# Hashed attention and a feed-forward on one core: queries are turned ahead of additions on VectorE, and normalizing and converting move into the phase on columns

## The chip, the core and the metric

The kernel runs on one core of a Trainium2 chip. The metric is the device time of one execution in microseconds. The profile is one execution taken by the hardware profiler; its times run from the first instruction. PE is TensorE's matmul, PEld its weight load, DVE is VectorE, ACT ScalarE, POOL GpSimd, and SP the engine that issues most transfers.

## What is computed

First comes attention over 4 batches and 8 heads, 768 positions of 64 numbers each. A query sees only keys with the same 6-bit hash. The result is then the input of a feed-forward with a gated activation.

```python
q_bits = (np.einsum('bhsd,dk->bhsk', q, proj) > 0)     # k likewise; 6 bits make a bucket
mask = q_bucket[:, :, :, None] == k_bucket[:, :, None, :]
scores = scale * np.matmul(q, k.transpose(0, 1, 3, 2))
scores = np.where(mask, scores, -1000000000.0)
attn = np.exp(scores - np.max(scores, axis=-1, keepdims=True))
attn = attn / (np.sum(attn, axis=-1, keepdims=True) + 1e-09)
x = np.matmul(attn, v)                                 # then (B,H,S,D) -> (B*S, H*D)
h = x @ w_in                                           # 3072x512 by 512x2048
out = (h * (1.0 / (1.0 + np.exp(-1.702 * h)))) @ w_out
```

## The kernel before

The kernel has two stages. The attention takes two heads at a time: a pair, one on partitions 0 to 63 and the other on 64 to 127. There are 16 pairs. The feed-forward follows; it multiplies matrices by a scheme of seven products in place of eight, and the change doesn't touch it.

Within a pair `n` the attention goes through these steps. The order of the calls is the order of the instructions on TensorE, VectorE, ScalarE and GpSimd (`manual_schedule`); each engine works through its own list in order and waits for the others by semaphores.

```python
def turn(n, name):                     # k or q, positions by features -> features by positions
    xt = xts[n, name] = wk.tile([P, S], F32, tag=f"{name}T", name=f"{name}T")   # 2 buffers
    nc.vector.transpose(xt, x.rearrange("p s i -> p (s i)"))

def hashed(n):                         # L408: four matmuls, on four groups of 32 columns of the array
    h = dots[n] = mps.tile([P, HS], F32, tag="m", name="hash")
    for i, x in enumerate("kq"):
        for c in range(2):
            r0 = D * i + 32 * c
            nc.tensor.matmul(h[r0 : r0 + 32, :], pf[x], xts[n, x][:, c * HS : (c + 1) * HS], ...)

def featured(n):                       # L413: bits as large numbers; eight small DMAs put them in place
    nc.vector.tensor_scalar(f, dots.pop(n), above[:, 0:1], weight[:, 0:1], op0=Alu.is_gt, op1=Alu.mult)
    ...
            queue.dma_start(out=feats[n % 2][x][...], in_=f[r0 : r0 + 2 * NB, :])

def scores(n, c, kts):                 # L432, L433; the feature product makes hidden scores very low
    for kt in kts:
        ps = sps.tile([P, 2, 512], F32, tag="s", name="ps")                    # 3 buffers
        ...                            # features (bf16), then queries by keys (f32)
        nc.scalar.activation(es[c][:, kt, :, 0:HS], ps[:, :, 0:HS], Act.Exp, scale=1.0 / D**0.5)

def add_low(n, c):                     # L440, L441: GpSimd adds three of six blocks of exponentials
    acc = accs[n, c, 0] = st.tile([P, 2, HS], F32, tag="acc0", name="acc0", bufs=1)
    nc.gpsimd.tensor_tensor(acc, es[c][:, 0, :, 0:HS], es[c][:, 1, :, 0:HS], op=Alu.add)
    nc.gpsimd.tensor_tensor(acc, acc, es[c][:, 2, :, 0:HS], op=Alu.add)

def add_high(n, c):                    # L446, L448: VectorE adds the other three, and GpSimd's sum
    nc.vector.scalar_tensor_tensor(acc, e[0], T * TINY, e[1], op0=Alu.add, op1=Alu.add)
    for x in (e[2], accs.pop((n, c, 0))):
        nc.vector.tensor_tensor(acc, acc, x, op=Alu.add)

def values(n, c, kts): ...             # L458: values by exponentials, in two halves c of the columns
def unload(n, c): ...                  # L469, L470: ScalarE writes them to xT
def total(n): ...                      # L479: sums over the keys, dn, four matmuls on four column groups

def invert(n):                         # 1/sum, laid out along the positions
    nc.vector.transpose(rt..., accs.pop(n))            # L485, reads dn
    nc.vector.reciprocal(r, ...)                       # L487, and L491 four times
    nc.vector.transpose(rs..., r...)                   # L493

def norm(n):                           # L498
    nc.vector.tensor_tensor(x, x, rs.rearrange("p (t s) -> p t s", t=T), op=Alu.mult)
```

Beside this a generator `convert` turns one block of the float64 weight `w_in` into float32. Each `step` issues one VectorE instruction of it, six in all: L178, L182, L186 (ahead of which ScalarE squares the high word, L190, once L182 has read it), L193, L195, L198.

The loop over the pairs, from the second on:

```python
for n in range(1, last + 1):
    scores(n, 0, every)
    add_low(n, 0)
    if n == 1:
        add_high(0, 1); turn(2, "k"); total(0)
    invert(n - 1)
    norm(n - 1)
    if 1 < n < last:
        turn(n + 1, "k")
    scores(n, 1, every)
    add_low(n, 1)
    add_high(n, 0)
    if n < last:
        turn(n + 1, "q")
        hashed(n + 1)
        featured(n + 1)
        ...                            # ScalarE measures k and q, for a guard on large inputs
    else:
        guard(0); guard(1)
    step(n, 2)
    add_high(n, 1)
    values(n, 0, every); unload(n, 0)
    step(n, 4)
    values(n, 1, every); unload(n, 1)
    total(n)
    ...                                # transfers: k and q of n + 2, v and a weight block of n + 1
```

So TensorE's order in a pair is twelve score blocks (72 instructions), the hash of the next pair (8), the values (48), dn (8). The raw k and q have one buffer each; a transfer into it waits until the turn and the measurement of the pair before have read it.

Of the kernel before, what the change touches and what calls it, by code (L numbers as in the profile page):

```python
# [38 lines left out]
def kernel(  # L39
# [243 lines left out]
    def attention(ff):  # L283
# [4 lines left out]
        with actx:  # L288
# [99 lines left out]
            def turn(n, name):  # L388
                x = raws[n, name]
                xt = xts[n, name] = wk.tile([P, S], F32, tag=f"{name}T", name=f"{name}T")  # L390
                nc.vector.transpose(xt, x.rearrange("p s i -> p (s i)"))  # L391

            def measure(n, name):

                x = raws.pop((n, name))
                i = 2 * n + "kq".index(name)
                junk = st.tile([P, S], BF16, tag="junk", name="junk", bufs=1)
                nc.scalar.activation(junk, x.rearrange("p s i -> p (s i)"), Act.Square, accum_out=sizes[:, i : i + 1])
# [3 lines left out]
            def hashed(n):  # L402
# [5 lines that stand above are left out]
                        nc.tensor.matmul(h[r0 : r0 + 32, :], pf[x], xts[n, x][:, c * HS : (c + 1) * HS],  # L408
                                         start=True, stop=True)

            def featured(n):
                f = wk.tile([P, HS], BF16, tag="f", name="f", bufs=1)
# [4 lines that stand above are left out]
                        queue = nc.scalar if (n, x, c) == (1, "q", 0) else nc.sync  # L417
                        for j in range(2):
                            r0 = D * i + 32 * c + 2 * NB * j
                            queue.dma_start(out=feats[n % 2][x][D * j : D * j + 2 * NB, c * HS : (c + 1) * HS],  # L420
                                            in_=f[r0 : r0 + 2 * NB, :])

            def scores(n, c, kts):
                qT, kT, qf, kf = xts[n, "q"], xts[n, "k"], feats[n % 2]["q"], feats[n % 2]["k"]
                cols = slice(c * HS, (c + 1) * HS)
                for kt in kts:
                    ps = sps.tile([P, 2, 512], F32, tag="s", name="ps")
                    keys = slice(kt * P, (kt + 1) * P)
                    for a, m, last in ((kf, qf, False), (kT, qT, True)):
                        for j in range(2):  # L430
                            hs = slice(D * j, D * (j + 1))
                            nc.tensor.matmul(ps[:, j, 0:HS], a[hs, keys], m[hs, cols], start=not last, stop=last)  # L432
                    nc.scalar.activation(es[c][:, kt, :, 0:HS], ps[:, :, 0:HS], Act.Exp, scale=1.0 / D**0.5)  # L433
# [3 lines left out]
            def add_low(n, c):  # L437
# [5 lines that stand above are left out]
            def add_high(n, c):  # L443
                e = [es[c][:, GT + i, :, 0:HS] for i in range(GT)]
                acc = accs[n, c] = st.tile([P, 2, HS], F32, tag="acc", name="acc")
# [3 lines that stand above are left out]
# [12 lines left out]
            def x_of(n):  # L461
                b, hp = pairs[n]
                x = xT[:, hp, b * S : (b + 1) * S]
                return x.rearrange("d (t p) -> d t p", p=P) if n else x.rearrange("d (p t) -> d t p", p=P)

            def unload(n, c):
                av = avs.pop((n, c))
                vs = st.tile([P, 1], F32, tag="vs", name="vs")
                nc.scalar.copy(vs, av[:, HS : HS + 1])  # L469
                nc.scalar.activation(x_of(n)[:, c * GT : (c + 1) * GT, :], av[:, 0:HS].rearrange("p (t s) -> p t s", t=GT), Act.Identity, bias=vs[:, 0:1])  # L470

            def total(n):

                dn = accs[n] = aps.tile([P, HS], F32, tag="av", name="dn")
                for c in range(2):
                    acc = accs.pop((n, c))
                    for j in range(2):
                        r0 = D * j + 32 * c
                        nc.tensor.matmul(dn[r0 : r0 + 32, :], ones[:, 0:32], acc[:, j, :], start=True, stop=True)  # L479

            def invert(n):


                rt = st.tile([P, HS // 32, 32], F32, tag="rt", name="rt", bufs=1)
                nc.vector.transpose(rt.rearrange("p s i -> p (s i)"), accs.pop(n))  # L485
                r = st.tile([P, 2, HS // 32], F32, tag="r", name="r")
                nc.vector.reciprocal(r, rt[:, :, 0].unsqueeze(1).to_broadcast([P, 2, HS // 32]))  # L487
                for r0 in range(0, P, 32):
                    c = r0 // 32 % 2
                    r1 = r0 + 32 - 64 * c  # L490
                    nc.vector.reciprocal(r[r1 : r1 + 32, c], rt[r0 : r0 + 32, :, 0])  # L491
                rs = accs[n] = st.tile([P, S], F32, tag="rs", name="rs", bufs=1)
                nc.vector.transpose(rs.rearrange("p (s i) -> p s i", i=32),  # L493
                                    r.rearrange("p c s -> p (c s)").unsqueeze(2).to_broadcast([P, S // 32, 32]))

            def norm(n):
                x, rs = x_of(n), accs.pop(n)
                nc.vector.tensor_tensor(x, x, rs.rearrange("p (t s) -> p t s", t=T), op=Alu.mult)  # L498

            last = len(pairs) - 1  # L500
            conv = {}

            def step(n, count=1):
                for _ in range(count):
                    next(conv.get(n, iter(())), None)
# [9 lines left out]
            def guard(part):  # L515
                if part == 0:
                    nc.vector.tensor_reduce(largest, sizes, axis=AX.X, op=Alu.max)
                else:
                    row = mps.tile([1, P], F32, tag="m", name="row")
                    nc.tensor.transpose(row, largest, ident)  # L520
                    nc.vector.tensor_reduce(largest[0:1, 0:1], row, axis=AX.X, op=Alu.max)
# [30 lines left out]
# [4 lines that stand above are left out]
                    add_high(0, 1)  # L556
                    turn(2, "k")
                    total(0)
                invert(n - 1)
                norm(n - 1)  # L560
                if 1 < n < last:
                    turn(n + 1, "k")
                scores(n, 1, every)
                add_low(n, 1)
                add_high(n, 0)
                if n < last:
                    turn(n + 1, "q")
                    hashed(n + 1)
                    featured(n + 1)
                    for x in "kq":  # L570
                        measure(n + 1, x)
                else:
                    guard(0)
                    guard(1)
                step(n, 2)
                add_high(n, 1)
                values(n, 0, every)
                unload(n, 0)
                step(n, 4)
                values(n, 1, every)  # L580
                unload(n, 1)
                total(n)
                if n + 2 <= last:
                    for x in "kq":
                        fetch(n + 2, x)
                if n < last:
                    fetch_v(n + 1)
                    begin(n + 1)
                if n > last - len(x_sums):
                    x_sums[n - last - 1]()  # L590
            for f in in_sums(0):
                f()
            early.close()
            next(ff)
            invert(last)
            norm(last)


# [370 lines left out]
    def whole(steps):  # L969
        for _ in steps:  # L970
            pass
# [46 lines left out]
```

## Time and profile before

| what | us |
|---|---|
| time, median of three runs | 888.33 |
| the three runs | 886.65 to 888.75 |
| span of the profiled execution | 886.9 |
| attention, to the end of the last dn | 335.4 |
| first product of the feed-forward (L705) | 288.6 |
| second product and the output | 262.9 |

The granted TensorE clock averages 0.995 of full speed. In the attention TensorE is busy 330.6 us of 335.4, VectorE 280.7, ScalarE 214.5 and GpSimd 123.6. In the feed-forward's first product TensorE is busy all of the 288.6 us.

The views used are the page (busy times, shares, the costliest groups), the chain of work that ended last in order of time, the timeline (each row a start, a length, an engine, a line, and in brackets the idle time before it with what ended it) and busy times by stretch. A matmul's busy time runs up to the next matmul where the two follow closely, so a wait inside a group of matmuls can show only as a longer group.

### The profile page before, as it was taken

The page shows a single profiled execution, that of the slowest core. Times are in us where ns is not written, and L with a number is a line of the kernel's source. Part 1 is how long each engine was busy: PE and PEld are TensorE (multiplying, and loading weights), DVE is VectorE, ACT ScalarE, POOL GpSimd, SP SyncE. Part 2 cuts the span into 40 slices and gives each one's busy share as a digit, 9 for nine tenths or more (in the row PEclk, how much of TensorE's full clock was granted, in tenths as well). Part 3 has the DMA queues.
Part 4 walks back from the last instruction along what each step waited for, and adds up shares of the span by engine and source line. Part 5 has one row for each costly group of instructions (what it writes and reads, how often), then busy time and mean ns, then how long its engine had stood idle before and what let it go on. Part 6 is the DMA issues. An engine that isn't in the chain of part 4 may idle for free.

```text
span 886.9 us, 11860 instructions
## 1 busy us (share of the span) xinstructions
PE 873.2 (98%) x4077; PEld 502.7 (57%) x4077; DVE 722.4 (81%) x1020; ACT 313.9 (35%) x519; POOL 319.0 (36%) x275
## 2 busy tenths in 40 slices
PE   9999999999999999999999999999999999999996
PEld 4444444444444444444444444444888888888885
DVE  4568989999998997777787786898797977897786
ACT  5746566666666652332222323222100000000000
POOL 4234333334334346666444435559913100000000
PEclk9999999999999999999999999999999999999998
DMA  5334444555544402555555545565845585477524
GB/s 131 58 57 81 82 83 82 94 97 99 110 83 82 82 27 84 202 182 198 190 195 201 191 161 199 198 219 197 296 183 190 167 223 214 163 221 238 198 97 98
DMA packets 169157, 132.00 MB, mean 149 GB/s; under 512 B 123617, under 2 KB 138113, under 8 KB 163713
## 3 DMA queue, kind: packets, MB, share of 16 engines
q1 hardware_dynamic: 166528, 129.70, 50.7%
q10 hardware_dynamic: 2560, 1.46, 0.8%
q8 instruction: 34, 0.56, 0.3%
q14 instruction: 35, 0.28, 0.1%
HBM read 79.69 MB, written 50.33 MB: 147 GB/s over the span
## 4 chain that ended last, share of the span: by engine, by line
PE 94%; DVE 4%; issue 1%; DMA 0%; ACTq 0%; DVEq 0%; ACT 0%
PE product L705 33%; PE product L817 27%; PE ps L432 16%; PE av L458 14%; PE hash L408 2%; PE dn L479 1%; DVE xT L821 1%; PE tp L366 1%; DVE y L797 1%; DVE acc L448 0%; DVE acc L446 0%; DMA k<-in_k_dram 0%; PE hash L373 0%; DVE rs L493 0%; DVE qT L391 0%
## 5 line engine op out<-in xcount | busy, mean ns | idle before, releaser
L433 ACT ACTIVATE e<-ps 128x768 f32<-128x768 f32 x192 | 151.5, 812 | 24.3 <-PE ps L432 21.9
L432 PE MATMUL ps<-qT,kT 64*128 64x384 f32 x768 | 155.1, 482 | 0.0
L705 PE MATMUL product<-xT,w_in_sb 128*128 128x512 f32 x288 | 135.4, 592 | 0.0
L458 PE MATMUL av<-e,v 128*64 128x385 f32 x768 | 129.1, 491 | 0.0
L440 POOL TENSOR_TENSOR acc<-e 128x768 f32<-128x768 f32 x32 | 49.3, 1541 | 206.6 <-ACT e L433 155.5
L713 ACT ACTIVATE c<-c 128x512 f32<-128x512 f32 x72 | 45.4, 630 | 186.2 <-issue 71.8
L458 PEld LDWEIGHTS av<-e,v 128*64 128x64 f32 x768 | 54.0, 136 | 74.1 <-issue 70.7
L705 PEld LDWEIGHTS product<-xT,w_in_sb 128*128 128x128 f32 x288 | 54.6, 190 | 69.0 <-issue 64.5
L705 PE MATMUL product<-t_x,s_in 128*128 128x512 f32 x192 | 90.2, 592 | 0.0
L432 PEld LDWEIGHTS ps<-qT,kT 64*128 64x128 f32 x768 | 68.0, 187 | 38.7 <-issue 38.7
L219 POOL TENSOR_TENSOR v<-c,u 128x512 f32<-128x512 f32 x24 | 34.2, 1425 | 123.3 <-ACT c L713 123.3
L830 ACT COPY u<-product 128x256 f32<-128x256 f32 x21 | 7.8, 373 | 172.1 <-PE product L817 138.9
L441 POOL TENSOR_TENSOR acc<-acc,e 128x768 f32<-128x768 f32 x32 | 62.7, 1960 | 2.5
L432 PE MATMUL ps<-qf,kf 64*128 64x384 bf16 x384 | 62.8, 324 | 0.1
L705 PEld LDWEIGHTS product<-t_x,s_in 128*128 128x128 f32 x192 | 36.5, 190 | 45.9 <-issue 43.3
L705 PE MATMUL product<-xT,s_in 128*128 128x512 f32 x96 | 45.1, 592 | 0.0
L705 PE MATMUL product<-t_x,w_in_sb 128*128 128x512 f32 x96 | 45.1, 592 | 0.0
L446 DVE SCALAR_TENSOR_TENSOR acc<-e 128x768 f32<-128x768 f32 x32 | 40.3, 1261 | 5.1 <-ACT e L433 5.1
L432 PEld LDWEIGHTS <-kf 64*128 64x128 bf16 x384 | 18.8, 94 | 35.1 <-issue 11.1
L469 ACT COPY vs<-av 128x1 f32<-128x1 f32 x32 | 5.1, 159 | 89.2 <-PE av L458 89.2
L817 PE MATMUL product<-raw_g,xT 128*128 128x256 f32 x152 | 35.1, 379 | 0.0
L448 DVE TENSOR_TENSOR acc<-acc,acc 128x768 f32<-128x768 f32 x32 | 31.0, 969 | 3.7 <-DVE acc L448 0.5
(207 smaller groups left out, 1535.4 us busy)
## 6 DMA issues: line engine op xcount, KB each, us to landing
raw_g<-g_dram SPq DMA_DIRECT2D x22, 1024.0 KB
s_in<-g_dram SPq DMA_DIRECT2D x20, 1024.0 KB
g_dram<-c SPq DMA_DIRECT2D x72, 256.0 KB
g_dram<-t SPq DMA_DIRECT2D x48, 256.0 KB
raw<-in_moe_w_in_dram SPq DMA_DIRECT2D x16, 512.0 KB
raw<-in_moe_w_out_dram SPq DMA_DIRECT2D x16, 512.0 KB
v<-in_v_dram SPq DMA_DIRECT2D x32, 192.0 KB
g_dram<-u SPq DMA_DIRECT2D x24, 256.0 KB
```

What stands on the lines that cost most here:

```text
L219: return [lambda: eng.tensor_tensor(t1, b12, b11, op=Alu.subtract), lambda: eng.tensor_tensor(b12, b22, b12, op=Alu.subtract), lambda: eng ...
L408: nc.tensor.matmul(h[r0 : r0 + 32, :], pf[x], xts[n, x][:, c * HS : (c + 1) * HS], start=True, stop=True)
L432: nc.tensor.matmul(ps[:, j, 0:HS], a[hs, keys], m[hs, cols], start=not last, stop=last)
L433: nc.scalar.activation(es[c][:, kt, :, 0:HS], ps[:, :, 0:HS], Act.Exp, scale=1.0 / D**0.5)
L440: nc.gpsimd.tensor_tensor(acc, es[c][:, 0, :, 0:HS], es[c][:, 1, :, 0:HS], op=Alu.add)
L441: nc.gpsimd.tensor_tensor(acc, acc, es[c][:, 2, :, 0:HS], op=Alu.add)
L446: nc.vector.scalar_tensor_tensor(acc, e[0], T * TINY, e[1], op0=Alu.add, op1=Alu.add)
L448: nc.vector.tensor_tensor(acc, acc, x, op=Alu.add)
L458: nc.tensor.matmul(av[D * j : D * (j + 1), :], vt[:, t, j, :], es[c][:, t, j, :], start=(t == 0), stop=(t == T - 1))
L705: nc.tensor.matmul(ps, wq[LEFT[i]][:, kc, :], xq[RIGHT[i]][:, kc, :], start=(kc == 0), stop=(kc == K2 - 1))
L713: nc.scalar.activation(c, c, Act.Gelu_apprx_sigmoid)
L817: nc.tensor.matmul(ps, wq[LEFT[i]][:, c, :], gq[RIGHT[i]][:, c, :], start=(c == 0), stop=(c == F4 - 1))
```

## The change

VectorE's order within a pair is changed. The first transpose of `invert` stays at the front, so that dn's buffer comes free; then the keys are turned, then the rest of `invert` runs. The queries of the next pair are turned ahead of the first additions. `norm` moves behind the hash and its features, and all six steps of the conversion move behind the second additions, that is, into the time in which TensorE multiplies values. The aim is that the turned queries, which TensorE's hash needs, don't stand behind work that nobody waits for. No instruction is added or left out, and the order of the other engines stays. In the last pair, which has no next one, norm moves behind the guard.

```diff
@@ invert @@
                 nc.vector.transpose(rt.rearrange("p s i -> p (s i)"), accs.pop(n))
+                yield
                 r = st.tile([P, 2, HS // 32], F32, tag="r", name="r")
...
@@ the loop over the pairs @@
-                invert(n - 1)
-                norm(n - 1)
+                inverted = invert(n - 1)
+                next(inverted)
                 if 1 < n < last:
                     turn(n + 1, "k")
+                whole(inverted)
                 scores(n, 1, every)
                 add_low(n, 1)
+                if n < last:
+                    turn(n + 1, "q")
                 add_high(n, 0)
                 if n < last:
-                    turn(n + 1, "q")
                     hashed(n + 1)
                     featured(n + 1)
...
                 else:
                     guard(0)
                     guard(1)
-                step(n, 2)
+                norm(n - 1)
                 add_high(n, 1)
                 values(n, 0, every)
                 unload(n, 0)
-                step(n, 4)
+                step(n, 6)
                 values(n, 1, every)
                 unload(n, 1)
                 total(n)
...
-            invert(last)
+            whole(invert(last))
             norm(last)
```

`whole` runs a generator to its end. For n = 1 the keys of pair 2 are turned ahead of `total(0)` in both kernels.

## The prediction

> **What bounds the kernel now.** I read the page first: busy times, then the engines of the chain that ended last.
>
> ```profile
> PE 873.2 (98%) x4077; PEld 502.7 (57%) x4077; DVE 722.4 (81%) x1020; ACT 313.9 (35%) x519; POOL 319.0 (36%) x275
> ...
> PE 94%; DVE 4%; issue 1%; DMA 0%; ACTq 0%; DVEq 0%; ACT 0%
> ```
>
> TensorE is the bound, and a reordering on VectorE (DVE) can pay only where TensorE is held up or runs below its rate. "Busy 98%" hides such places, because a matmul's end is modelled and stretches up to the next one. So I read the chain in order of time (start, length, what) and compared the length of the same work in different places.
>
> ```profile
> 23.45 0.78 PE hash L408 x8
> ...
> 45.06 1.49 PE hash L408 x4
> 46.56 8.76 PE av L458 x48
> ...
> 196.36 9.80 PE ps L432 x72
> 206.15 1.49 PE hash L408 x8
> 207.64 7.92 PE av L458 x48
> 215.56 0.78 PE dn L479 x8
> ```
>
> The eight hash instructions took 0.78 us at 23.45, where keys and queries were both ready, but 1.49 at 206.15. The four sums into dn, with the same shapes and the same four column groups, always take 0.78. So 0.71 us is lost in the hash of a pair in the steady state. A pair there takes 9.80 + 1.49 + 7.92 + 0.78 = 19.99 us, and this repeats from n = 2 to 14. Only n = 4 to 5 is longer, with one period about 0.35 us over.
>
> The timeline of that stretch names the holder (start, length, then the idle time before and its releaser):
>
> ```profile
> 199.41 1.96 DVE L498 TENSOR_TENSOR xT<-xT,rs 128x768 f32<-128x768 f32 x1
> ...
> 205.78 0.97 DVE L391 STREAM_TRANSPOSE qT<-q 128x768 f32<-128x768 f32 x1
> 206.00 1.54 POOL L440 TENSOR_TENSOR acc<-e 128x768 f32<-128x768 f32 x1 [3.08 <-DVE acc L448]
> 206.08 0.14 PEld L408 LDWEIGHTS hash<-kT,pf_k 128*32 128x32 f32 x4 [0.55 <-DVE acc L448]
> ...
> 206.80 0.14 PEld L408 LDWEIGHTS hash<-qT,pf_q 128*32 128x32 f32 x4 [0.58 <-DVE qT L391]
> ...
> 207.69 0.68 DVE L413 TENSOR_SCALAR f<-hash,above,weight 128x384 bf16<-128x384 f32 x1 [0.94 <-PE hash L408]
> ```
>
> The turn of q ends at 206.75 and the q half of the hash starts at 206.80. The k half was through by then, so the halves run one after the other. The turn stands behind three additions, and those behind the normalization.
>
> The first pair of the loop, n = 1, is worse. I cut its 19.58 us by clock (us, busy, granted clock, DMA share, GB/s):
>
> ```profile
> 35.74:41.41 5.67, 5.67 (x46) 1.00 0.31 63
> 41.41:45.06 3.65, 0.84 (x6) 0.97 0.02 4
> 45.06:46.50 1.44, 1.44 (x6) 0.50 0.00 0
> 46.50:50.50 4.00, 4.00 (x22) 0.78 0.03 7
> 50.50:55.32 4.82, 4.82 (x34) 1.00 0.18 33
> ```
>
> TensorE stands for 2.8 us before the q half, and then it runs at half clock to about 48.
>
> **What the Trainium skill says.** "TensorEngine Tiling (Array Packing)", Key Properties: tiles work independently and in parallel. The 0.78 against 1.49 agrees: four column tiles together take about as long as two. "TensorE: Matmul & The Clock Gate", What's actually happening: the array falls to half clock after an idle window of some 3.4 us and needs a busy one to return. The 0.50 after 2.8 us of standing agrees in kind; the idle time here is shorter. "SBUF — State Buffer", Who interferes with whom: a VectorE instruction with two SBUF inputs contends with a GpSimd one that reads SBUF, one with a single input doesn't. The trace agrees: beside GpSimd's additions the normalization took 1.96 us and the first addition 1.54 (0.95 alone), while the turn of k at 201.29 kept its 0.96.
>
> **The change, part by part.** No instruction is added or removed; only VectorE's order differs (ScalarE, GpSimd and TensorE keep theirs).
>
> *Order within a pair.* Before: rt, r, rs, norm, kT, three additions, qT, f, two conversion steps, three additions, four conversion steps. After: rt, kT, r, rs, qT, three additions, f, norm, three additions, six conversion steps.
>
> *Steady state, TensorE.* Measured from the end of dn, qT is done after 0.1 + 0.58 + 0.96 + 0.30 + 0.92 + 0.98 + 0.97 = 4.8 us and gaps, say 5. TensorE asks for it 9.80 us after dn. Even 4 us of lag doesn't hold it, so the hash falls to 0.78 and the period to 9.80 + 0.78 + 7.92 + 0.78 = 19.28. Pairs n = 2 to 14 hash a next one: 13 x 0.71 = 9.2 us.
>
> *n = 1.* The inversion runs from 36.59 to 39.49. The turn of q(2) can follow at once and end at 40.5: its transfer was issued at 30.0 to 32.2, and the DMA share falls to 0.02 from 38 us. The hash, due at 41.41, then ends at 42.19, the values take 7.92 without the slow clock, and dn starts at 50.1 instead of 55.3: 5.2 us. (2.8 standing, 0.7 for the overlap, 0.75 slow hash, 0.9 slow values.) The second additions must be through for dn. On VectorE: first additions to 43.6, f to 44.3, norm (1.56) to 45.9, additions (1.2 + 0.96 + 0.96) to about 49.3, after GpSimd's sum at about 46.9. That is in time by 0.8.
>
> *n = 4 and 15.* The late period (0.35) and the last dn (1.07 instead of 0.78, waiting for an addition) go too: 0.6 us.
>
> *What I add back.* The period of 19.28 comes close to VectorE's own. Its busy time from 196.42 to 216.41 sums to 18.7, and 0.35 of gaps makes 19.05. The change moves L178 out of GpSimd's way (1.57 to about 0.69), so I estimate 18 to 19: it fits, with little room. The second loop is the transfer: from the end of f, 6.1 us to issue eight feature DMAs, then k with 2.2 us of issue. The 393 KB of k, counted at the rates 129, 172, 175 GB/s from 195.6, are across at 198.1: 9.7 after f's end at 188.39. Behind that kT 1.0, r and rs 2.3, qT 1.0, additions 3.6, f 0.7: 18.3, and up to 19.4 if completion takes a microsecond more. So f may slide by 0.1 to 0.3 us a pair. The first 1 to 1.5 us cost nothing: the additions for dn have 7.2 us after f and need 5.6. Estimate of the loss: 0.7 us.
>
> The sum: 9.2 + 5.2 + 0.6 - 0.7 = 14.3; 888.3 - 14.3 = 874.0 us, 1.6% less. From 335 us on the kernel is the same: 288.6 us of TensorE without a gap, then the second product.
>
> **The rivals.** *VectorE becomes the bound.* For it: the busy sum of 18.7 in 19.99, and normalization that may still meet GpSimd's addition, now right after f. If its period came to 19.7, only 0.28 x 13 = 3.7 of the 9.2 us would remain, and with n = 1 the time would be about 879. Against it: 0.94 us of idle ahead of f, and two long overlaps with GpSimd become one or one and a half.
>
> *The transfer of k takes the place of the wait.* kT now comes after 0.6 us of the pair instead of 5, and everything behind it waits too, since VectorE works in order. For it: k is across 1.8 us after dn's end at 196.3. Against it: the q turn has 4 us of room, f's features about 3. If completions lie well over a microsecond behind the last byte, the period is 19.5 to 19.8 and the time 876 to 880.
>
> *The exponentials are held up.* The square of the weights on ScalarE (L190) waits for L182, now about 1 us before dn rather than 5 after the hash; the last unload and the next pair's exponentials stand behind it. With six such 0.6 us slips the loss would be 4 us: 878. Against it: three score buffers allow TensorE 2.4 us, and the square should be done 0.3 us before dn ends.
>
> *No effect.* If the hash were long for another reason (the switch of tile shapes, say), only n = 1 would gain: 883. The 0.78 at 23.45 speaks against it.
>
> **Range and chances.** Low end: no loss, and the shortest of the three runs before was 1.7 under the median: 871.5. High end: one rival in half its strength, 878.5. Two per cent less is 870.6, which needs more than every loss I found. Faster by over 2%: 0.05. Within 2%: 0.93. Slower: 0.02, for a wait I didn't see.
>
> **What would show it.** Right: hash at 0.78 in the chain from n = 2 to 14, and periods of 19.3; no stretch near 45 us at clock 0.50, dn of n = 1 near 50; dn of the last pair near 320 instead of 334.3; idle time of VectorE ahead of f, released by the hash; kT with up to 2 us of idle before it. Wrong: periods of 19.6 or more with dn waiting for an addition (VectorE or the transfer), ps waiting for e (ScalarE), or a longer stretch after the attention.

## The result, and the profile after

| | median us | runs, from to |
|---|---|---|
| before | 888.54 | 886.65 to 888.82 |
| after | 877.48 | 876.77 to 877.59 |

The ratio is 0.9878, with a 95% interval of 0.9861 to 0.9895: 11 us less. The predicted 874.0 was 3.5 us too low; the range of 871.5 to 878.5 holds the result. The span of the profiled execution fell from 886.9 to 875.0.

The page of the changed kernel, the lines that answer to those shown of before: busy times, and the engines of the chain that ended last.

```profile
PE 861.9 (99%) x4077; PEld 502.7 (57%) x4077; DVE 719.6 (82%) x1020; ACT 310.2 (35%) x519; POOL 321.3 (37%) x275
...
PE 90%; DVE 6%; SPq 1%; DMA 1%; issue 1%; ACT 0%; ACTq 0%; DVEq 0%
```

TensorE's busy time fell by 11.3 us although it executes the same 4077 instructions: what went away is the time in which the two halves of the hash ran one after the other, each booked as work, and 1.6 us of work at half clock. VectorE has a larger part of the chain than before, a first sign that it now ends some waits. The chain in order of time (start, length, what) says where:

```profile
35.48 0.78 PE dn L479 x8
...
46.60 2.23 DVE acc L446
...
50.99 0.84 PE dn L479 x4
51.84 9.80 PE ps L432 x72
61.63 0.78 PE hash L408 x8
62.41 7.92 PE av L458 x48
70.33 0.78 PE dn L479 x8
...
313.67 0.11 DVE largest L518
313.81 0.27 PE row L521
314.09 7.92 PE av L458 x48
322.00 0.78 PE dn L479 x8
322.78 288.60 PE product L708 x672
```

(The dn at 35.48 is that of n = 0.) Three things are to be seen. The hash takes 0.78 us in place of 1.49, and a pair takes 9.80 + 0.78 + 7.92 + 0.78 = 19.28. The dn of the first pair of the loop comes at 50.99, in two halves: the line shown is the second one, and VectorE's additions (L446, L448) lead up to it. And near 313.7 the chain passes from VectorE's L518 to TensorE: a new wait. The feed-forward's first product takes 288.60 us as before.

Where the time came from, from one dn to another: from the first dn to the end of the last took 335.36 - 35.74 = 299.6 us before and 322.78 - 35.48 = 287.3 after. Of these 12.3 us, 9.2 come from thirteen hashes, 4.0 from the pair n = 1 (19.58 to 15.58), 0.6 from the late period and the last dn, and 1.5 were lost at L518.

The clock in the pair n = 1, to compare with the stretches shown of before (us, busy, granted clock, DMA share, GB/s):

```profile
41.20:45.00 3.80, 3.80 (x30) 1.00 0.01 4
45.00:46.50 1.50, 1.50 (x12) 1.00 0.05 12
46.50:50.50 4.00, 4.00 (x26) 1.00 0.05 12
```

TensorE no longer stands, and the clock stays at 1.00. But the timeline of the same pair shows what follows:

```profile
43.61 1.54 POOL L440 TENSOR_TENSOR acc<-e 128x768 f32<-128x768 f32 x1 [7.12 <-DVE acc L448]
...
43.98 2.62 DVE L499 TENSOR_TENSOR xT<-xT,rs 128x768 f32<-128x768 f32 x1
...
45.23 2.77 POOL L441 TENSOR_TENSOR acc<-acc,e 128x768 f32<-128x768 f32 x1
...
46.42 2.39 DVE L446 SCALAR_TENSOR_TENSOR acc<-e 128x768 f32<-128x768 f32 x1
...
50.99 0.84 PE L479 MATMUL dn<-acc,ones 128*32 128x384 f32 x4 [0.31 <-DVE acc L448]
```

VectorE and GpSimd take turns by whole instructions: the normalization waits for L440 to end, L441 then for the normalization, L446 for L441. So normalization and the first addition took 5.0 us together in place of my 2.8, the additions ended at 50.94 in place of 49.3, and the second half of dn waited 0.31 us after the first. It then ran by itself for 0.84 us, where both halves together take 0.78: 1.1 us lost in all.

The last pair, at the row of the guard:

```profile
307.83 0.57 DVE L485 STREAM_TRANSPOSE rt<-dn 128x384 f32<-128x384 f32 x1
...
313.58 0.18 DVE L518 TENSOR_REDUCE largest<-sizes 128x1 f32<-128x32 f32 x1
...
313.81 0.27 PE L521 MATMUL row<-ident,largest 128*1 128x128 f32 x1 [1.52 <-DVE largest L518]
```

VectorE begins this pair (rt) 5.4 us after the dn before it. In the middle pairs it begins 2 to 3 us after dn, because the conversion now all stands behind the additions; here L221, a sum for the feed-forward, comes on top, and takes 2.57 us beside GpSimd. L518 stands behind the three first additions, and TensorE waits 1.52 us for it.

### The profile page after: what moved, and what is told of

Read it like the earlier page. It is cut to its first block, busy times and chain, and to the rows that moved or that the text cites. A ratio compares the mean times of both kernels' runs of the same rounds, so it can differ in the third digit from the quotient of the medians.

```text
span 875.0 us, 11818 instructions
## 1 busy us (share of the span) xinstructions
PE 861.9 (99%) x4077; PEld 502.7 (57%) x4077; DVE 719.6 (82%) x1020; ACT 310.2 (35%) x519; POOL 321.3 (37%) x275
## 4 chain that ended last, share of the span: by engine, by line
PE 90%; DVE 6%; SPq 1%; DMA 1%; issue 1%; ACT 0%; ACTq 0%; DVEq 0%
PE product L708 33%; PE product L820 27%; PE ps L432 16%; PE av L458 12%; PE dn L479 1%; PE hash L408 1%; DVE acc L448 1%; DVE acc L446 1%; DVE xT L824 1%; SPq L420 1%; DVE y L800 1%; DVE xT L499 1%; DMA pj<-in_proj_dram 0%; DMA k<-in_k_dram 0%; DVE t_x L221 0%
## 5 line engine op out<-in xcount | busy, mean ns | idle before, releaser
L433 ACT ACTIVATE e<-ps 128x768 f32<-128x768 f32 x192 | 149.0, 813 | 15.7 <-PE ps L432 13.7
L440 POOL TENSOR_TENSOR acc<-e 128x768 f32<-128x768 f32 x32 | 50.4, 1575 | 192.2 <-ACT e L433 113.4
L441 POOL TENSOR_TENSOR acc<-acc,e 128x768 f32<-128x768 f32 x32 | 64.1, 2002 | 2.5
L446 DVE SCALAR_TENSOR_TENSOR acc<-e 128x768 f32<-128x768 f32 x32 | 52.1, 1628 | 5.1 <-ACT e L433 5.1
L448 DVE TENSOR_TENSOR acc<-acc,e 128x768 f32<-128x768 f32 x32 | 31.0, 969 | 3.8 <-ACT e L433 0.5
L448 DVE TENSOR_TENSOR acc<-acc,acc 128x768 f32<-128x768 f32 x32 | 31.0, 969 | 3.3
```

## The experiments

Times are medians; ratios, with their 95% intervals, are to the kernel before on the same chip, which took 888.1 to 888.9 us beside these runs. A period is the time from the end of one dn to the end of the next; steady pairs of the changed kernel have 19.28 us.

**e1: only the turn of q.** The kernel before, with

```diff
+                if n < last:
+                    turn(n + 1, "q")
                 add_high(n, 0)
                 if n < last:
-                    turn(n + 1, "q")
                     hashed(n + 1)
```

> The kernel before with one part of the change: the turn of the next queries moves ahead of the first additions; normalization and conversion stay where they were. Theory (the turn of q is all that TensorE waits for): from the end of dn the turn ends after some 7 us, still ahead of the 9.8 us at which the hash is due, so hash 0.78 us in nearly all pairs, 13 x 0.71 = 9.2 us; for n = 1 the turn ends near 42.1, TensorE stands under 1 us and keeps its clock, about 4.4 us; sum 13.6, some 875 us. Rival (VectorE becomes the bound unless normalization and conversion get out of GpSimd's way): the period goes to about 19.6 instead of 19.28, a third to a half of the gain is lost, 879 to 881 us, and dn waits for additions.

Measured: 882.01 us, ratio 0.9936 (0.9916 to 0.9957). The hash is at 0.78 from n = 2 on, so the theory holds for TensorE's wait; but only 6 of the 11 us come. Its timeline, VectorE in a steady pair and what dn waits for:

```profile
201.33 0.67 DVE L413 TENSOR_SCALAR f<-hash,above,weight 128x384 bf16<-128x384 f32 x1
201.92 1.73 DVE L178 SCALAR_TENSOR_TENSOR w_in_sb<-raw,mask_3fffffff 128x512 uint32<-128x512 uint32 x1
203.69 2.06 DVE L182 SCALAR_TENSOR_TENSOR bits<-raw,w_in_sb 128x512 uint32<-128x512 uint32 x1
205.67 0.95 DVE L446 SCALAR_TENSOR_TENSOR acc<-e 128x768 f32<-128x768 f32 x1
...
208.79 0.14 PEld L479 LDWEIGHTS dn<-acc,ones 128*32 128x32 f32 x4 [0.29 <-DVE acc L448]
```

The features no longer wait for the hash: VectorE works without a pause, period 19.70. The two conversion steps meet GpSimd (1.73 and 2.06 in place of 0.69 each) ahead of the additions, and the second half of dn waits in every pair. The rival is what happened, and a little more of it than it said: with the hash fast, VectorE's order behind it sets the period.

**e2: the turn of q undone.** The changed kernel with that same part back.

> The changed kernel with that one part undone: the queries are turned behind the first additions again; keys, normalization and conversion stay in their new places. Theory (the turn of q is what matters): VectorE begins a pair some 2 us after dn's end, the turn then ends about 9.9 us after dn or later, so the hash is near 1.49 us again in most pairs, and n = 1 keeps some 3 us of its gain; 883 to 887 us. Rival (moving normalization and conversion is what frees TensorE): the hash stays at 0.78 and the time at 877 to 879 us.

Measured: 884.61 us, ratio 0.9961 (0.9950 to 0.9972). The hash is 1.02 to 1.49 us from n = 7 on, since the turn ends at about the moment at which TensorE asks, and 1.65 to 2.2 in n = 2 to 6, where the periods are 20.2 to 20.7. The theory holds and the rival falls, but the turn is late for another reason than in the kernel before. VectorE waits for k, here in a middle pair:

```profile
196.44 0.98 DVE L391 STREAM_TRANSPOSE kT<-k 128x768 f32<-128x768 f32 x1 [1.66 <-DMA k<-in_k_dram]
```

From the end of one f to that of the next it is exactly the period, in every pair: 10.9 to 12.1 us until k is in place, then 8.60 to the end of f. That is the circle which e5 names below. Either half of the change alone gives a third to a little over a half of it.

**e3: two conversion steps back.** The changed kernel with

```diff
                 norm(n - 1)
+                step(n, 2)
                 add_high(n, 1)
...
-                step(n, 6)
+                step(n, 4)
```

> The changed kernel with the first two conversion steps ahead of the second additions again. Theory (that part is worth nothing; it only moves the meeting with GpSimd from one instruction to another): L178 goes from 0.69 to about 1.57 us and the second L446 from 2.43 to about 0.95 us, the additions end in time for dn, 876.5 to 878 us as the changed kernel; the wait of the last pair shrinks by some tenths. Rival (the additions for dn need the conversion out of their way): dn waits 0.3 to 0.5 us in every pair, 881 to 884 us.

Measured: 879.50 us, ratio 0.9909 (0.9882 to 0.9936), 2.0 us above the changed kernel, between the two. L178 took 2.17 us, more than my 1.57, as it waits for the whole of L441. dn waits for additions in eight more pairs (0.8 us in n = 2, 1.3 in the last, where the row in turn no longer waits, and under 0.1 to 0.7 in the others), not in all. The conversion's move is worth about 2 us, and through dn.

**e4: the guard's reduction ahead.** The changed kernel; in the last pair

```diff
                 if n < last:
                     turn(n + 1, "q")
+                else:
+                    guard(0)
                 add_high(n, 0)
```

and without `guard(0)` at its old place.

> The changed kernel, in the last pair with the first reduction of the guard (it reads only the measured sizes) ahead of the first additions instead of behind them. In the changed kernel TensorE stands 1.5 us there, because VectorE begins that pair 5.4 us after dn. Theory (that wait is on the path to the end): TensorE's row follows the scores without a gap, the last dn comes 1.5 us earlier, 875.9 to 876.2 us. Rival (the feed-forward then waits for VectorE's conversion and sums instead): the same time, 877.5 us, with a gap in the first product.

Measured: 876.32 us, ratio 0.9869 (0.9842 to 0.9896), the runs from 875.88 to 878.10. Two of the four runs are where they were expected (875.88 and 875.89) and one is at 876.75, but the profiled one is that of 878.10 and can't show them. In it the row no longer waits, but a transfer of q came late in n = 14, VectorE ran later still, and dn of the last two pairs waited for additions. So it is open from this run how much the row alone is worth.

**e5: normalization back in front.** The changed kernel with `norm(n - 1)` right behind `whole(inverted)`.

> The changed kernel with normalization back in front, ahead of the turn of q; the conversion stays behind the second additions. With the first and third run this splits what the two moves are worth. Theory (the conversion's place counts for dn, the normalization's hardly: the turn of q still ends some 8.8 us after dn, ahead of the hash at 9.8): hash 0.78 throughout, 877.5 to 879.5 us, the wait ahead of the last pair's row grows to 2 to 3 us. Rival (normalization in front is what made VectorE the bound in the first run): dn waits in most pairs and the time is 881 to 883 us.

Measured: 889.89 us, ratio 1.0021 (1.0009 to 1.0033): the whole gain is gone. Neither theory had this. dn waits only about 0.2 us a pair, not the half microsecond and more of the rival, and the period is 19.7 in the middle pairs, 20.2 to 20.8 in n = 2 to 6, 21.1 in n = 13 and 14, and 23.4 in the last. The hash takes up to 2.3 us: it waits for q again. VectorE in a middle pair:

```profile
186.29 0.67 DVE L413 TENSOR_SCALAR f<-hash,above,weight 128x384 bf16<-128x384 f32 x1
...
198.04 0.98 DVE L391 STREAM_TRANSPOSE kT<-k 128x768 f32<-128x768 f32 x1 [0.94 <-DMA k<-in_k_dram]
...
201.27 0.96 DVE L499 TENSOR_TENSOR xT<-xT,rs 128x768 f32<-128x768 f32 x1
202.15 0.97 DVE L391 STREAM_TRANSPOSE qT<-q 128x768 f32<-128x768 f32 x1
...
206.00 0.67 DVE L413 TENSOR_SCALAR f<-hash,above,weight 128x384 bf16<-128x384 f32 x1
```

f ends at 186.96, k is in place at 198.04, 11.1 us later; from there to the next end of f are 8.6. This makes a circle of 19.7 us: the features' eight issues stand ahead of k's, k's turn ahead of everything on VectorE, and that ahead of the next features. Normalization at that place is about 1 us more in the circle. In the changed kernel it is outside, and from k's turn to the end of f are 7.5 us where f doesn't wait for the hash (n = 2 to 6). So the same circle is 11.1 + 7.5 = 18.6 in the middle pairs, under TensorE's 19.28. In n = 3 to 5, where k takes 11.8 us, it is 19.3: there the changed kernel has no slack left. The prediction had this circle as its second rival, at 18.3 to 19.4. I formed the theory anew: e5's pairs up to n = 12 are bound by the circle, not by the amount of VectorE's work. Of the 15.2 us that its trace loses against the changed kernel in the attention, 6.0 lie in n = 2 to 6, where k takes 11.6 to 12.2 us, 2.6 in the six middle pairs and 6.9 in the last three, where the sums for the feed-forward come on top and VectorE doesn't wait for k; n = 1 gains 0.3.

**e9: k's turn behind normalization**, and **e10: k's transfer earlier.** Both are e5 with one thing moved, and both open the circle, one on VectorE and the other on the queue.

```diff
 e9, on e5
-                inverted = invert(n - 1)
-                next(inverted)
-                if 1 < n < last:
-                    turn(n + 1, "k")
-                whole(inverted)
+                whole(invert(n - 1))
                 norm(n - 1)
+                if 1 < n < last:
+                    turn(n + 1, "k")
 e10, on e5
                     hashed(n + 1)
+                    for x in "kq":
+                        measure(n + 1, x)
+                    if n + 2 <= last:
+                        fetch(n + 2, "k")
                     featured(n + 1)
```

> The fifth run with one instruction moved: the turn of k comes behind normalization instead of right behind the first transpose, so the inversion and normalization fill the time in which k is under way. The instructions are the same. In the fifth run the period was 19.7 us = 11.1 (end of f to k in place) + 8.6 (turn of k to the end of f). Theory (that loop through the transfer is the bound of the fifth run): it shrinks to about 11.1 + 5.8 = 16.9, the wait for k goes, and VectorE's own work is left as a bound near 19.3 to 19.6: 878 to 882 us. Rival (normalization in front is itself too much work for VectorE at that place): 888 to 890 us.

> The fifth run with VectorE's order untouched and only the transfer moved: the four issues of k come behind the first of the eight feature transfers instead of behind all. Theory (the loop through k's transfer bounds the fifth run): k is in place some 5 us sooner, VectorE doesn't wait for it, the period falls to near 19.3, 877 to 880 us. Rival (VectorE's order alone makes the fifth run slow): 888 to 890 us, or more, as the features come 2.2 us later.

Measured: e9 880.92 us, ratio 0.9909 (0.9883 to 0.9935); e10 877.74, ratio 0.9878 (0.9852 to 0.9904). In both the wait of k's turn is gone and the period is 19.28, in e9 from n = 2 to 13, in e10 from n = 3 to 14. e10 has e5's order on VectorE unchanged, so that order by itself isn't what made e5 slow, nor its last pairs; the circle is shown. e10's timeline: k is issued 0.8 us after the features begin, and its turn follows rt with no wait.

```profile
198.31 0.74 SPq L420 DMA_DIRECT2D kf<-f  x1
199.15 2.17 SPq L328 DMA_DIRECT2D k<-in_k_dram  x4
...
207.72 0.58 DVE L485 STREAM_TRANSPOSE rt<-dn 128x384 f32<-128x384 f32 x1
208.22 0.94 DVE L391 STREAM_TRANSPOSE kT<-k 128x768 f32<-128x768 f32 x1
```

e9 is 3 us behind e10 because of its last two pairs: n = 14 takes 1.8 us too long, and in the last the row waits 2.9 us for L518. In its middle pairs VectorE has no idle time and the period is still 19.28, so my estimate of its limit there (19.3 to 19.6) was a little high. The limit itself isn't known: L446 and L448 take 2.0 and 2.25 us beside GpSimd, 0.92 and 0.96 alone, so waits are booked as work.

**e6: normalization behind the second additions.** The changed kernel with

```diff
-                norm(n - 1)
                 add_high(n, 1)
+                norm(n - 1)
```

> The changed kernel with normalization behind the second additions instead of ahead of them. Theory (in the first pair of the loop dn waits because normalization and the first addition stand in front of it, each behind a whole GpSimd instruction): dn of that pair comes without its gap, about 1.1 us earlier; the row of the last pair still waits 1.5 us; 876.2 to 876.8 us. Rival (VectorE's lag is the same whatever the order, and the gain is given back in the last pair): 877.2 to 877.8 us.

Measured: 875.06 us, ratio 0.9851 (0.9833 to 0.9870). The pair n = 1:

```profile
44.36 2.00 DVE L446 SCALAR_TENSOR_TENSOR acc<-e 128x768 f32<-128x768 f32 x1
...
48.82 0.96 DVE L448 TENSOR_TENSOR acc<-acc,acc 128x768 f32<-128x768 f32 x1
49.69 1.58 DVE L499 TENSOR_TENSOR xT<-xT,rs 128x768 f32<-128x768 f32 x1
...
50.24 0.16 PEld L479 LDWEIGHTS dn<-acc,ones 128*32 128x32 f32 x8 [0.60 <-issue]
```

The collisions with GpSimd are still there (L446 2.00), but normalization no longer stands ahead of the additions: they end at 49.78, and dn comes whole at 50.24. The pair takes 14.43 us. The time is 1.1 us under what was expected. A part of that I hadn't foreseen: VectorE reaches L221 at a better moment (1.22 us in place of 2.57 beside GpSimd) and begins the last pair 3.7 us after dn in place of 5.4, so the row hardly waits. From dn to dn the trace gains 1.1 us in n = 1 and 1.4 in the last pair. It gives 1.1 back in n = 3 and 4 (periods of 20.06 and 19.56): there the square of the weights waits for L182 and the exponentials for the square, until TensorE waits 0.6 us for one of them. So its trace shows 1.5 us of the 2.4 by which the medians differ. The waits in n = 3 and 4 are the prediction's third rival, small and real.

**e7: the new order in n = 1 alone.** The kernel before, with `turn(2, "q")` ahead of the additions and `norm(0)` behind the features in that pair only.

> The kernel before with the new order in its second pair alone (n = 1: q turned ahead of the additions, normalization behind the features); all later pairs as before. It measures the second term of the prediction's sum by itself. Theory (the terms add; that pair is worth 4.0 us and the thirteen hashes 9.2): 884.0 to 884.9 us, no stretch at clock 0.50 there, hash 1.49 us in the later pairs. Rival (the earlier start is lost again, because the features or keys of the next pair come too late): 886.5 to 888 us.

Measured: 884.99 us, ratio 0.9962 (0.9948 to 0.9976), some 3.5 us less. In its trace that pair takes 15.58 us from dn to dn, exactly as in the changed kernel, the clock is 1.00 throughout it, and the hash behind it 1.49. So this term is worth 4.0 us by itself. The next pairs don't lose it again; n = 13 takes 21.11 us in this trace, 1.1 more than in that of the kernel before, for a reason that no run separates.

**e8: e6 and e4 together**, and **e11: with e10's transfer as well.**

> The sixth and the fourth run together: normalization behind the second additions, and in the last pair the guard's first reduction ahead of the first additions. Theory (the two waits that kept the changed kernel from its sum lie at different places and add): 1.1 + 1.5 us less than the changed kernel, 874.6 to 875.2 us. Rival (in the last pair dn then waits for the additions instead, as VectorE begins it late): 876 to 876.6 us.

> The eighth run and the tenth's transfer together: normalization behind the second additions, the guard's first reduction ahead in the last pair, and k issued behind the first feature transfer. Theory (in the eighth run TensorE has only small waits left, some of them because VectorE waits 0.4 to 1 us for k in most pairs and then runs late): up to 0.8 us less than the eighth run, 874.2 to 875.1 us. Rival (nothing is left in the attention but TensorE's own work, and features that come 2.2 us later hold the scores up): 875.1 to 877 us.

Measured: e8 875.11 us, ratio 0.9854 (0.9837 to 0.9871); e11 873.74, ratio 0.9831 (0.9817 to 0.9845). e8 is where it was expected, but no faster than e6, which had already lost most of the row's wait: the guard's place adds nothing that shows. e11 has the lowest median of all, under both kernels; its gain over e8 is within the intervals, and the traces don't show it where the theory put it. From the end of the first dn to that of the last e11 takes 284.7 us and e8 284.5: the 0.75 us that e8 lost in n = 3 and 4 are gone, but n = 2 takes 20.28, a microsecond more. What e11's profiled execution gains lies in the feed-forward, which it doesn't change.

## Why the prediction was right, and where its sum was off

*Steady state.* Right in mechanism and size: 0.78 us of hash, 19.28 us a pair. e1 and e2 show the turn of q as the cause: with it alone the hash is short from n = 2 on, without it long again. e1 is the cleaner of the two, as in e2 the circle through k makes the turn late. What e1 lacks is the room that the two other moves make on VectorE.

*"No instruction is added; VectorE has room."* Right by little, and for a reason that I had half wrong. L178 fell to 0.69 us as I said, but the meeting with GpSimd didn't go, it moved: the second L446 went from 0.95 to 2.43. VectorE was busy 88.87 us in five pairs after and 90.83 before. The "18.7" of busy time in a pair added lengths of instructions that overlap; the stretch from 196.42 to 216.41 shows 18.18. And a part of such busy time is waiting for GpSimd, so neither figure is VectorE's limit.

*n = 1, 5.2 us.* Mechanism right (no standing, full clock), size off: 4.0. The mis-sized term is "norm (1.56), additions (1.2 + 0.96 + 0.96)"; normalization took 2.62 and the first addition 2.39. I had taken both from a trace in which they met GpSimd differently. With normalization out of the way, in e6, dn comes in time and the pair takes 14.43 us, 5.1 less than before: the 5.2 was right but for this term.

*"What I add back", 0.7 us.* The failed term. The slide of f cost under 0.1 us in the steady pairs, but VectorE began the last pair 5.4 us late, and the guard's reduction, which the prediction doesn't mention, made TensorE wait 1.52 us. I had counted VectorE's work in a steady pair and not looked at the end, where from n = 12 on a sum for the feed-forward comes on top in each pair.

*The sum.* Of the 14.3 us predicted the traces show 12.3 in the attention: 1.2 are missing in n = 1, and 0.8 at L518. The medians differ by 11.1. Of the rest 0.7 us lie at the feed-forward's end (below); the remainder is between the profiled executions and the medians.

*The rivals.* VectorE as the bound and the transfer of k were both near: the first is what e1 shows, the second is e5 and e2. In the middle pairs k was in place 11.1 us after f's end, 1.4 later than the bytes alone said, and the way from k's turn to f took 7.5 in place of the 8.6 that the prediction added up. The two misses nearly cancel, so its 18.3 for this circle came out near the 18.6 by luck; in n = 3 to 5 it was 19.3, and nothing was left. ScalarE's square did wait for L182 (3.0 us at 205.26) but held TensorE up only in e6.

What stays open: the feed-forward's end differs by 0.7 us between the two profiled executions (24.3 us from the last full product to the end before, 24.9 after). It lies within the spread of the runs. Over the thirteen profiles, the time behind the last dn is 551.3 to 551.5 us in six, the kernel before and e11 among them, and 552.0 to 552.5 in seven, the changed kernel and e8 among them. No experiment aimed at it, and the cause stays open. Open is also why k takes 11.6 to 12.2 us in the first pairs and 11.1 in the middle ones.

## What to carry to other kernels

Before moving work off an engine's path, look for the circle that it closes: here features, a transfer queue and a turn made a loop of 18.6 to 19.3 us under a bound of 19.3, and one microsecond of harmless normalization on it ate the whole gain. When two engines take turns, a reordering moves the collision to another instruction, so ask which instruction it lands on and who waits for that one. And a change of order that leaves an engine without slack shows its cost at the ends of the loop, in the first and last pass, not in the steady one.

## What the runs showed of the hardware

VectorE instructions with two inputs in SBUF and GpSimd's additions take turns by whole instructions, in both directions. The changed kernel's steady pair shows a full sequence: L499 waits for L440, L441 for L499, and L446 for L441.

```profile
197.06 1.54 POOL L440 TENSOR_TENSOR acc<-e 128x768 f32<-128x768 f32 x1 [4.27 <-DVE acc L448]
...
198.08 1.34 DVE L499 TENSOR_TENSOR xT<-xT,rs 128x768 f32<-128x768 f32 x1
...
198.68 2.27 POOL L441 TENSOR_TENSOR acc<-acc,e 128x768 f32<-128x768 f32 x1
...
199.34 2.43 DVE L446 SCALAR_TENSOR_TENSOR acc<-e 128x768 f32<-128x768 f32 x1
```

L440 ends at 198.60 and L499 0.82 later; L441 ends 1.53 after that, at 200.95; L446 ends 0.82 after L441. A waiting instruction is booked as busy.

TensorE's clock in n = 1 of the kernel before (us, busy, granted clock, DMA share, GB/s):

```profile
44.00:44.80 0.80, 0.00 (x0) 1.00 0.00 0
44.85:48.20 3.35, 3.13 (x10) 0.50 0.00 0
48.25:50.00 1.75, 1.75 (x14) 1.00 0.04 11
```

The k half of the hash had ended at 42.25, so the clock fell to half after some 2.6 us of standing, while TensorE still stood. It was full again 3.4 us later, and the slow work added 1.6 us (hash 0.75, values 0.84).
